# A written-out step order replaced behind its 114th step, in an attention and ELU-MLP kernel

## The chip, the cores and the metric

The kernel runs on one core of one Trainium2 chip. The metric is the device time in microseconds (us), as the median of several runs. One more execution was recorded by the hardware profiler; its instructions, waits and DMA landings are the trace that this document reads.

## The reference

Attention over 8 batches and 8 heads with 576 queries of width 64, causal over 576 keys, and with 16 further "beacon" keys and values per head that every query sees. The heads are put side by side, which gives 4608 tokens of width 512, and these go through a two-layer MLP with an ELU between the layers.

```python
def _attn_ref(q, k, v, beacon_k, beacon_v):
    k_all = np.concatenate([beacon_k, k], axis=2)
    v_all = np.concatenate([beacon_v, v], axis=2)
    scores = scale * np.matmul(q, k_all.transpose(0, 1, 3, 2))
    causal[:, Nb:] = np.triu(np.ones((S, S), dtype=bool), k=1)
    scores = np.where(causal, -1000000000.0, scores)
    ...                                    # softmax over the last axis
    return np.matmul(a, v_all)

x = attn_out.transpose(0, 2, 1, 3).reshape(4608, 512)
h = x @ w_in                               # 512 -> 2048
g = np.where(h > 0.0, h, np.exp(np.minimum(h, 0.0)) - 1.0)
out = g @ w_out                            # 2048 -> 512
```

## The kernel before

The whole kernel is a list of 1554 short steps, written out in one string that `run` goes through. Each step is a small function that issues a few instructions, and a word such as `F.4.11` calls step F with the arguments 4 and 11. No scheduler moves anything afterwards: every engine (PE for matmuls, DVE, ACT, POOL, and SP, which only issues DMAs) executes its own instructions in the order of the list, and stands still while the first of them waits. What a step needs of another engine is held by semaphores that the tile library sets from tiles, their buffers and the order of the list.

Steps by batch b (0 to 7), the attention:

- `lq` (batches 0 to 2) loads q and k with a cast to bf16, and `T`, `cq`, `ck` transpose them on PE and copy them to SBUF. From batch 3 on `lk.b.n` (line 795) copies q (n = 0) or k (n = 1) with a cast into a DRAM scratch tile of its own, and `lt.b.x` (line 802, on SP) brings one half of the heads (x = 0 or 1) back by two DMA transposes, into qst1 (x = 0) or kst1 (x = 1). `lp.b.x` (lines 810 and 811, on POOL) puts the beacon keys and zeros beside them: one memset and one copy.
- `lv.b.j` loads a block of v (line 147; block 0 brings the beacon rows too, line 152). `wi` and `wo` load w_in and w_out. All loads but those of `lt` are issued by POOL, since they cast, and go through one DMA queue (q0). A load also waits on a semaphore for the load eight places ahead of it.
- `S.b.g` (line 330) computes 512 columns of scores into one of two PSUM tiles, `x` (line 345, ACT) takes their exponential, `m` (line 350, DVE) masks them. `D.b.g.n` (line 410) adds blocks on DVE ahead of the sums; `L` computes the softmax sums and part of the product with v, `n` (ACT) their reciprocals, `W` the rest of the product (line 390), `M` (lines 488, 498, 505) scales it into xT, the input of the MLP.

Steps by token tile t (two of 256 tokens, then eight of 512), the MLP:

- `F.t.i` (line 528) computes 512 columns of the first layer into one of two PSUM banks; `e` (line 538) and `u` (line 543) take exponential and ReLU on ACT, `k` (line 553) joins them to the ELU on DVE. Early tiles use `r` and `g` (lines 560 and 566, both DVE) in place of `u` and `k`.
- `G` (line 575) is the second layer of tiles 0 and 1, with `o` and `s` to copy and store. From tile 2 on it is a Strassen-like form with seven products: `Z` and `wt` (line 596, DVE) make sums of activations and weights, `Q.t.a.b` (line 650) issues the matmuls a to b of 112, `J` (lines 664, 668, 671) collects and stores, `Jh` the last two.
- From tile 4 on a part of the first layer has that form as well: `H` and `X` make the sums, `P` (line 732) the products, `K` (lines 742, 745) collects, and `E`, `U`, `V` (lines 754, 761, 771) make the ELU.

The list's order sets everything that can be moved: what POOL issues when, what stands behind what on each engine, and which work is at hand when an engine comes free. Around batch 3, POOL's own order in the list before is

```
lk.3.0 lv.2.0 lk.3.1 lk.4.0 lk.5.0 lv.2.2 lv.2.1 lp.3.1 lv.2.3 lv.3.0 lp.3.0 lk.4.1 lk.7.0 lv.3.1 lv.3.4 lk.6.1
```

and SP's `lt.3.0 s.0.0 lt.3.1 s.0.1 lt.4.0`.

Of the kernel before, what the change touches and what calls it, by code (L numbers as in the profile page):

```python
# [17 lines left out]
def kernel(  # L18
# [837 lines left out]
    wt.3.0 u.2.10 G.1.1.3 M.2.1.0 e.2.8 D.3.0.0 e.2.10 S.3.6 S.3.9 o.1.1 x.3.6 k.2.10 x.3.9 F.2.6
    r.2.8 e.2.6 W.2.1 u.2.6 lv.3.2 k.2.2 S.3.10 lv.3.3 g.2.8 F.2.11 M.2.1.1 F.3.0 x.3.10 o.1.0
    e.2.11 u.2.11 lv.4.0 S.3.8 u.3.0 k.2.6 k.2.11 e.3.0 m.3.0.1 S.3.12 F.3.3 Z.2.3.1 x.3.12 Z.2.3.0
    Z.2.1.1 e.3.3 x.3.8 D.3.0.1 F.3.4 Q.2.0.7 e.3.4 lp.4.0 u.3.4 Q.2.7.14 S.3.11 Z.2.1.0 S.3.7 u.3.3
    Q.2.14.21 J.2.0.v x.3.11 s.0.1 lp.4.1 x.3.7 F.3.13 F.3.14 k.3.4 k.3.3 Q.2.21.28 Z.2.2.0 lv.4.4  # L860
    lt.4.0 e.3.13 S.4.4 Z.2.2.1 u.3.13 S.4.1 lt.4.1 u.3.14 D.3.0.2 D.3.0.3 Q.2.28.35 wt.4.1 lk.5.1
    x.4.4 F.3.8 m.3.1.0 k.3.0 m.3.1.1 x.4.1 e.3.14 s.1.0 L.3.0 W.3.0 F.3.2 n.3.0 k.3.14 M.3.0.0
    M.3.0.1 e.3.8 e.3.2 u.3.8 lv.4.3 Q.2.35.42 S.4.3 S.4.5 u.3.2 J.2.1 lv.4.1 Z.2.4.0 F.3.6 x.4.5
    k.3.8 x.4.3 wt.3.1 k.3.13 lv.4.2 Q.2.42.49 F.3.12 e.3.6 S.4.8 u.3.6 D.3.1.0 S.4.0 x.4.8 X.4.1
    H.4.1 k.3.2 Q.2.49.56 x.4.0 k.3.6 D.3.1.1 F.3.1 Q.2.56.63 u.3.12 J.2.2.v e.3.12 e.3.1 S.4.6
    D.3.1.2 u.3.1 k.3.12 S.4.2 x.4.2 D.3.1.3 F.3.7 x.4.6 F.3.9 e.3.9 lk.6.0 W.3.1 m.4.0.0 e.3.7
    H.3.0 u.3.7 u.3.9 L.3.1 k.3.1 Z.2.4.1 Q.2.63.70 D.4.0.0 k.3.9 F.3.15 n.3.1 M.3.1.1 e.3.15 u.3.15
    F.3.5 Q.2.70.77 M.3.1.0 u.3.5 e.3.5 S.4.12 lt.5.0 S.4.10 lv.5.3 F.3.11 k.3.7 J.2.3 x.4.10
    m.4.0.1 Q.2.77.84 F.4.7 u.3.11 e.3.11 H.4.0 F.3.10 D.4.0.1 k.3.11 x.4.12 k.3.5 J.2.4 S.4.11
    S.4.9 X.4.2 H.4.2 Q.2.84.91 D.4.0.2 e.4.7 Q.2.91.98 u.4.7 Q.2.98.105 e.3.10 J.2.5 P.4.0.0  # L870
    Z.3.3.0 u.3.10 x.4.11 X.4.3 lp.5.0 x.4.9 S.4.7 S.5.3 K.4.0.0 P.4.0.1 P.4.0.2 k.3.15 x.5.3
    K.4.0.1 k.3.10 Q.2.105.112 J.2.6.v P.4.0.3 x.4.7 Q.3.0.7 K.4.0.2 E.4.0.1 S.5.2 S.5.0 P.4.0.4
    K.4.0.3 X.4.4 lp.5.1 lt.5.1 m.4.1.1 k.4.7 x.5.0 P.4.0.5 Z.3.1.0 K.4.0.4 U.4.0.1 Q.3.7.14 x.5.2
    lv.5.4 Q.3.14.21 P.4.0.6 m.4.1.0 lk.7.1 S.5.4 D.4.0.3 U.4.0.6 K.4.0.5 V.4.0.1 E.4.0.6 S.5.5
    F.4.8 x.5.4 F.4.14 x.5.5 J.3.0.v e.4.8 Z.3.2.0 Q.3.21.28 e.4.14 V.4.0.6 u.4.14 L.4.0 W.4.0 u.4.8
    n.4.0 F.4.15 u.4.15 Z.3.3.1 Z.3.1.1 k.4.8 Z.3.4.0 k.4.14 M.4.0.0 F.4.6 Q.3.28.35 Z.3.2.1 e.4.15
    E.4.0.4 F.4.11 u.4.6 M.4.0.1 k.4.15 D.4.1.0 e.4.6 u.4.11 e.4.11 Q.3.35.42 S.5.9 S.5.1 F.4.13
    Z.3.4.1 x.5.9 J.3.1 k.4.11 U.4.0.4 F.4.12 Q.3.42.49 x.5.1 k.4.6 u.4.12 e.4.12 D.4.1.1 e.4.13
    u.4.13 k.4.12 Q.3.49.56 V.4.0.4 S.5.8 D.4.1.2 D.4.1.3 S.5.6 x.5.8 F.4.5 lp.6.0 x.5.6 lv.5.0
    u.4.5 F.4.9 m.5.0.0 Q.3.56.63 k.4.13 e.4.5 lt.6.0 L.4.1 n.4.1 J.3.2.v m.5.0.1 u.4.9 W.4.1 lv.6.3  # L880
    F.4.4 Q.3.63.70 k.4.5 e.4.9 M.4.1.0 lv.5.1 M.4.1.1 F.4.10 S.5.10 X.5.1 u.4.4 k.4.9 S.5.7 e.4.4
    F.5.12 Q.3.70.77 J.3.3 D.5.0.0 X.5.2 e.4.10 Q.3.77.84 E.4.0.5 k.4.4 u.4.10 x.5.7 X.5.4 lv.6.1
    e.5.12 u.5.12 P.5.0.0 x.5.10 Q.3.84.91 K.5.0.0 P.5.0.1 S.5.11 k.4.10 J.3.4 U.4.0.5 S.5.12
    Z.4.3.1 lp.6.1 K.5.0.1 D.5.0.1 P.5.0.2 Q.3.91.98 lt.6.1 Q.3.98.105 J.3.5 x.5.11 lv.5.2 X.5.3
    V.4.0.5 P.5.0.3 D.5.0.2 x.5.12 U.5.0.1 S.6.4 S.6.5 K.5.0.2 lv.6.4 m.5.1.0 x.6.5 Q.3.105.112
    K.5.0.3 P.5.0.4 x.6.4 Q.4.0.7 Z.4.3.0 D.5.0.3 P.5.0.5 K.5.0.4 J.3.6.v S.6.0 E.5.0.1 S.6.3
    Z.4.1.0 P.5.0.6 K.5.0.5 lv.6.2 x.6.3 U.5.0.6 Q.4.7.14 Z.4.2.0 E.5.0.6 L.5.0 n.5.0 F.5.6
    Q.4.14.21 F.5.13 k.5.12 V.5.0.1 e.5.6 m.5.1.1 x.6.0 Q.4.21.28 M.5.0.0 u.5.6 e.5.13 S.6.1 Z.4.1.1
    s.1.1 u.5.13 J.4.0.v S.6.2 V.5.0.6 x.6.2 F.5.4 Z.4.2.1 k.5.13 e.5.4 Q.4.28.35 u.5.4 F.5.15 x.6.1
    D.5.1.0 Q.4.35.42 u.5.15 e.5.15 k.5.6 D.5.1.1 D.5.1.2 F.5.5 lv.6.0 u.5.5 k.5.4 e.5.5 S.6.6 W.5.0  # L890
    J.4.1 k.5.5 U.5.0.5 Z.4.4.1 M.5.0.1 E.5.0.4 F.5.10 U.5.0.4 V.5.0.4 Q.4.42.49 x.6.6 Q.4.49.56
    lt.7.0 S.6.7 D.5.1.3 Z.4.4.0 E.5.0.5 x.6.7 S.6.10 J.4.2.v x.6.10 m.6.0.0 F.5.8 k.5.15 u.5.10
    u.5.8 Q.4.56.63 e.5.10 L.5.1 e.5.8 V.5.0.5 W.5.1 lv.7.1 Q.4.63.70 m.6.0.1 k.5.8 n.5.1 k.5.10
    F.5.14 e.5.14 F.5.7 M.5.1.0 u.5.14 u.5.7 lp.7.0 Q.4.70.77 J.4.3 e.5.7 M.5.1.1 D.6.0.0 S.6.11
    D.6.0.1 S.6.9 x.6.9 F.5.9 e.5.9 k.5.14 F.5.11 Z.5.3.0 u.5.9 x.6.11 e.5.11 X.6.1 u.5.11 X.6.2
    Q.4.77.84 F.6.9 S.6.12 S.6.8 D.6.0.2 lv.7.4 D.6.0.3 Q.4.84.91 J.4.4 F.6.12 X.6.3 x.6.12 x.6.8
    k.5.9 Q.4.91.98 k.5.7 e.6.12 m.6.1.0 S.7.4 u.6.9 S.7.3 Q.4.98.105 u.6.12 P.6.0.0 e.6.9 m.6.1.1
    P.6.0.1 x.7.4 K.6.0.0 Z.5.3.1 Z.5.1.0 x.7.3 J.4.5 Q.4.105.112 P.6.0.2 K.6.0.2 k.5.11 Q.5.0.7
    K.6.0.1 P.6.0.3 J.4.6.v X.6.4 S.7.1 S.7.2 E.6.0.1 U.6.0.1 k.6.9 K.6.0.3 P.6.0.4 x.7.1 Q.5.7.14
    k.6.12 lv.7.0 K.6.0.4 x.7.2 lt.7.1 Z.5.2.0 P.6.0.5 P.6.0.6 V.6.0.1 L.6.0 U.6.0.4 W.6.0 Q.5.14.21  # L900
    K.6.0.5 n.6.0 F.6.5 U.6.0.6 E.6.0.6 F.6.6 E.6.0.4 Q.5.21.28 D.6.1.0 e.6.6 D.6.1.1 u.6.6 M.6.0.1
    J.5.0.v M.6.0.0 Z.5.1.1 V.6.0.4 k.6.6 u.6.5 Z.5.2.1 e.6.5 lv.7.2 S.7.5 S.7.0 Q.5.28.35 x.7.0
    J.5.1 F.6.7 u.6.7 F.6.4 k.6.5 m.7.0.0 Q.5.35.42 e.6.7 k.6.7 u.6.4 F.6.14 Z.5.4.0 x.7.5 D.6.1.2
# [72 lines left out]
```

## Time and profile before

| | us |
|---|---|
| median of 3 runs | 333.67 (333.29 to 335.55) |
| the profiled execution, whole | 334.63 |
| its span, from the first to the last instruction | 332.9 |
| PE busy in it | 321.0 |
| DVE busy | 300.1 |
| ACT busy | 291.6 |
| POOL busy | 89.7 |
| step 115 (S.1.1) starts on PE | 26.6 |
| the last matmul ends | 329.4 |

The predicted time is one of the first row's kind; instruction times and waits are those of the profiled execution, counted from its span's start. The granted TensorE clock was 1.00 throughout. A wait is put down to what released it; "issue" means that the engine waited for nothing that the profile shows.

### The profile page before, as it was taken

The page shows a single profiled execution, that of the slowest core. Times are in us where ns is not written, and L with a number is a line of the kernel's source. Part 1 is how long each engine was busy: PE and PEld are TensorE (multiplying, and loading weights), DVE is VectorE, ACT ScalarE, POOL GpSimd, SP SyncE. Part 2 cuts the span into 40 slices and gives each one's busy share as a digit, 9 for nine tenths or more (in the row PEclk, how much of TensorE's full clock was granted, in tenths as well). Part 3 has the DMA queues.
Part 4 walks back from the last instruction along what each step waited for, and adds up shares of the span by engine and source line. Part 5 has one row for each costly group of instructions (what it writes and reads, how often), then busy time and mean ns, then how long its engine had stood idle before and what let it go on. Part 6 is the DMA issues. An engine that isn't in the chain of part 4 may idle for free. (4 is left out here: it accounts for less than half of the span.)

```text
span 332.9 us, 8762 instructions
## 1 busy us (share of the span) xinstructions
PE 321.0 (96%) x3572; PEld 213.9 (64%) x3575; DVE 300.1 (90%) x568; ACT 291.6 (88%) x481; POOL 89.7 (27%) x121
## 2 busy tenths in 40 slices
...
DMA  8999999999999993592999594510110021020123
GB/s 110 156 179 174 168 186 174 158 149 175 174 158 145 182 165 36 109 137 59 113 126 131 104 59 79 104 34 2 63 35 25 8 96 33 17 81 32 34 79 112
DMA packets 129080, 34.65 MB, mean 104 GB/s; under 512 B 112912, under 2 KB 127504, under 8 KB 129040
## 3 DMA queue, kind: packets, MB, share of 16 engines
q0 software_dynamic: 94912, 18.49, 67.8%
...
q10 hardware_dynamic: 576, 0.13, 0.2%
...
## 5 line engine op out<-in xcount | busy, mean ns | idle before, releaser
L345 ACT ACTIVATE et<-sc 128x1024 f16<-128x1024 f32 (+2 forms) x114 | 105.4, 982 | 2.8 <-PE sc L330 2.3
L528 PE MATMUL hps<-xT,w_in 128*128 128x512 f16 (+1 forms) x448 | 94.9, 349 | 3.6 <-DVE gt L566 2.1
L650 PEld LDWEIGHTS <-gt 128*128 128x128 f16 x768 | 74.2, 98 | 17.7 <-issue 1.9
L528 PEld LDWEIGHTS <-w_in 128*128 128x128 f16 x448 | 41.5, 98 | 37.6 <-issue 7.1
L538 ACT ACTIVATE e<-hps 128x512 f32<-128x512 f32 x96 | 58.3, 622 | 5.9 <-PE hps L528 3.4
L553 DVE SCALAR_TENSOR_TENSOR gt<-e,r 128x512 f16<-128x512 f32 x84 | 56.2, 683 | 1.4 <-ACT r L543 0.7
L543 ACT ACTIVATE r<-hps 128x512 f16<-128x512 f32 x84 | 51.0, 627 | 2.1 <-PE hps L528 1.2
L650 PE MATMUL ops<-w_out,gt 128*128 128x256 f16 x368 | 48.9, 273 | 0.0
L147 POOL DMA_DIRECT2D v<-in_v_dram x40 | 35.8, 949 | 46.9 <-PE ut L390 26.2
L650 PE MATMUL ops<-wt,gt 128*128 128x256 f16 x352 | 48.3, 273 | 0.0
L596 DVE TENSOR_TENSOR gt<-gt 128x1024 f16<-128x1024 f16 x48 | 32.6, 684 | 0.2
L771 DVE SCALAR_TENSOR_TENSOR gt<-e,r 128x512 f16<-128x512 f32 x48 | 32.1, 683 | 0.0
L350 DVE TENSOR_TENSOR et<-et,triu 128x1024 f16<-128x1024 f16 (+5 forms) x66 | 26.9, 447 | 0.5 <-ACT et L345 0.5
L390 PEld LDWEIGHTS <-v 128*32 128x32 f16 (+1 forms) x800 | 17.5, 96 | 10.3 <-issue 2.7
L742 ACT COPY kst<-hps 128x512 f32<-128x512 f32 x36 | 21.6, 601 | 1.9 <-PE hps L732 1.5
L390 PE MATMUL ut<-et,v 128*32 128x464 f16 (+3 forms) x560 | 20.9, 296 | 0.0
L732 PEld LDWEIGHTS <-w_in 128*128 128x128 f16 x192 | 18.4, 98 | 3.4 <-issue 1.2
L410 DVE TENSOR_TENSOR qk<-qk,et 128x1344 f16<-128x1344 f16 (+2 forms) x30 | 17.5, 585 | 0.3
L488 DVE TENSOR_TENSOR xT<-ut,rl 128x672 f16<-128x672 f32 (+12 forms) x26 | 16.4, 670 | 0.6 <-PE ut L390 0.4
L671 DVE TENSOR_TENSOR osb<-ops,sm 128x512 f32<-128x512 f32 x23 | 15.7, 684 | 1.3 <-PE ops L650 1.3
L575 PE MATMUL ops<-w_out,gt 128*128 128x512 f16 x64 | 16.4, 381 | 0.0
L650 PE MATMUL ops<-w_out,s 128*128 128x256 f16 x112 | 15.2, 273 | 0.0
(126 smaller groups left out, 495.2 us busy)
## 6 DMA issues: line engine op xcount, KB each, us to landing
...
```

The costliest lines, as they stand in the source:

```text
L147: nc.gpsimd.dma_start(out=vt[b][r0:r0 + n, j, :, :], in_=v[b, :, ilo[j]:ilo[j] + n, :].rearrange("h s d -> s h d"),)
L345: nc.scalar.activation(out=ets[b, d][:, :, a - EC2 * d:e - EC2 * d], in_=sc[b, g][:, :, a - c0:e - c0], func=AFT.Exp, bias=0.0, scale=SCALE)
L350: nc.vector.tensor_tensor(out=o, in0=o, in1=i, op=ALU.mult)
L390: nc.tensor.matmul(out=t[32 * i:32 * (i + 1), a - qa:e - qa], lhsT=ones[0:kc[j], :] if half is None else v16[0:kc[j], j, h, 32 * half:32 * ...
L528: nc.tensor.matmul(out=h[:, n_, :], lhsT=w_in16[:, cc, P * fc:P * (fc + 1)], rhs=xt[k][:, cc, a - TT * k:e - TT * k], start=(cc == 0), sto ...
L538: nc.scalar.activation(out=eb[t, i], in_=flat(hp[t, i]), func=AFT.Exp, bias=0.0, scale=1.0)
L543: nc.scalar.activation(out=rb[t, i], in_=flat(hp[t, i]), func=AFT.Relu, bias=0.0, scale=1.0)
L553: nc.vector.scalar_tensor_tensor(out=half(t, i), in0=eb[t, i], scalar=1.0, in1=rb[t, i], op0=ALU.subtract, op1=ALU.min)
L596: (nc.vector if eng == "v" else nc.gpsimd).tensor_tensor(out=o_, in0=a_, in1=b_, op=op_)
L650: nc.tensor.matmul(out=xy[t, n_][qd], lhsT=lw[:, P * qd:P * (qd + 1)], rhs=wt_[:, c, :], start=(first and c == 0 and (qd == 0 or (t, n_) n ...
L742: (nc.scalar.copy if eng == "s" else nc.vector.tensor_copy)(out=fm[t, g, ph], in_=src)
L771: eng.scalar_tensor_tensor(out=o_, in0=v_(eb[t, g, ph]), scalar=1.0, in1=v_(rb[t, g, ph]), op0=ALU.subtract, op1=ALU.min)
```

## The change

The first 114 steps stay. The 1440 steps behind them are put in another order: it has the same words, each as often, with the same engines, sizes, tiles and buffer counts. All engines' queues are reordered by it, the loads that POOL issues and the transposes that SP issues among them. In the new list steps of one kind follow each other more often (`F`, `e`, `u`, `k` of one block, all loads of one batch, the eight `D.2` adds with `H.1.2`, `H.2.0` to `H.4.2` near them), and many loads stand earlier. POOL's order around batch 3 becomes

```
wo.2 lk.3.0 wo.3 lk.3.1 lv.2.4 lv.2.0 lv.2.1 lk.6.0 lk.4.1 lv.2.2 lv.2.3 lk.4.0 lk.5.0 lk.7.0 lp.3.1 lp.3.0 lv.3.2 lv.3.0 lv.3.4 lv.3.1 lv.3.3 lk.6.1 lk.7.1 lk.5.1 lp.4.0
```

and SP's `lt.3.0 lt.3.1 s.0.0 s.0.1 s.1.0 lt.4.0`. The diff, cut to the stretch up to batch 3's first scores and to the end:

```diff
-    wh.4 F.0.1 e.0.1 S.1.1 r.0.1 g.0.1 S.1.4 x.1.4 F.0.0 S.1.2 F.0.2 x.1.1 x.1.2 u.0.0 lv.0.3 lv.0.4
-    lq.1.0.4.8 e.0.2 m.0.3.2 m.0.1.2 m.0.3.3 L.0.B n.0.B e.0.0 wi.1.0 wi.1.1 wi.1.2 wi.1.3 wi.1.4
-    wi.1.5 wi.1.6 wi.1.7 W.0.B.0 M.0.B.0 W.0.B.1 M.0.B.1 wo.0 r.0.2 T.1.2.0 F.1.1 ck.1.2.0 g.0.2
-    T.1.3.0 e.1.1 u.1.1 S.1.6 x.1.6 F.0.4 F.1.7 e.0.4 k.0.0 cq.1.3.0 cb.1.3 lq.2.0.0.8 S.1.0 r.0.4
-    S.1.12 e.1.7 g.0.4 r.1.7 F.0.5 x.1.0 S.1.7 g.1.7 x.1.12 H.1.1 cb.2.0 e.0.5 m.1.0.0 r.0.5 wo.1
-    lv.1.4 x.1.7 D.1.0.0 g.0.5 cb.2.2 lv.1.0 F.0.7 S.1.11 e.0.7 r.0.7 x.1.11 G.0.0.0 S.1.9 F.0.3
-    lv.1.1 g.0.7 x.1.9 S.1.10 u.0.3 e.0.3 k.1.1 S.1.8 F.1.6 F.1.3 G.0.1.0 x.1.8 lv.1.3 T.2.3.0 u.1.6
-    x.1.10 T.2.2.0 e.1.3 k.0.3 e.1.6 m.1.0.1 cb.2.1 D.1.0.1 ck.2.3.0 m.1.1.1 ck.2.2.0 m.1.1.0 u.1.3
-    F.1.0 H.1.0 lv.2.4 D.1.0.2 lv.1.2 T.2.1.0 S.2.7 G.0.1.1 D.1.1.0 F.1.2 x.2.7 e.1.0 cq.2.1.0 wo.3
-    D.1.1.1 wo.2 S.2.11 D.1.1.2 k.1.3 D.1.1.3 D.1.0.3 lk.3.0 u.1.0 S.2.12 x.2.11 F.0.6 lv.2.0 x.2.12
-    T.2.0.0 L.1.1 k.1.0 n.1.1 e.0.6 u.1.2 G.0.0.1 e.1.2 cq.2.0.0 M.1.1.0 W.1.1 r.0.6 M.1.1.1 k.1.6
-    g.0.6 W.1.0 L.1.0 F.1.5 F.1.4 n.1.0 lk.3.1 e.1.5 M.1.0.0 M.1.0.1 r.1.5 lk.4.0 e.1.4 r.1.4
-    G.0.1.2 S.2.5 g.1.4 x.2.5 S.2.4 x.2.4 G.0.0.2 lk.5.0 S.2.3 F.2.15 g.1.5 x.2.3 F.2.7 u.2.15
-    wt.1.0 S.2.6 e.2.15 S.2.2 x.2.6 lv.2.2 wt.2.0 lt.3.0 k.1.2 cb.2.3 wt.1.1 G.0.1.3 x.2.2 F.2.0
-    u.2.7 k.2.15 m.2.0.1 e.2.7 S.2.8 u.2.0 wt.2.1 e.2.0 o.0.1 S.2.0 G.0.0.3 x.2.0 F.2.3 F.2.9 lv.2.1
-    e.2.3 x.2.8 o.0.0 lp.3.1 k.2.7 r.2.3 e.2.9 lv.2.3 g.2.3 S.2.9 r.2.9 H.2.1 G.1.0.0 F.2.12 S.2.10
-    x.2.9 g.2.9 S.2.1 e.2.12 u.2.12 x.2.1 x.2.10 G.1.0.1 F.2.13 H.1.2 G.1.0.2 m.2.1.1 s.0.0 lv.3.0
-    F.2.5 u.2.13 k.2.12 e.2.13 lp.3.0 e.2.5 H.2.0 k.2.0 S.3.5 m.2.1.0 S.3.4 D.2.1.0 lk.4.1 G.1.1.0
-    x.3.5 lk.7.0 m.2.0.0 D.2.0.0 F.2.14 u.2.5 F.2.4 lv.3.1 x.3.4 lv.3.4 D.2.0.1 S.3.0 D.2.0.2 e.2.14
 ...
-    P.9.3.5 Q.9.0.8 V.9.2.5 K.9.3.4 P.9.3.6 U.9.3.1 U.9.3.4 K.9.3.5 J.8.5 U.9.3.5 E.9.3.5 E.9.3.6
-    V.9.3.1 Z.9.2.0 U.9.3.6 E.9.3.4 Q.8.98.105 V.9.3.5 Z.9.3.1 Q.9.8.16 Q.8.105.112 Q.9.16.24 J.9.0
-    V.9.3.6 V.9.3.4 Q.9.24.32 Q.9.32.40 Z.9.1.1 Z.9.2.1 J.9.1 Q.9.40.48 Q.9.48.56 Z.9.4.0 J.9.2
-    J.8.6 Q.9.56.64 Z.9.4.1 Q.9.64.72 J.9.3 Q.9.72.80 J.9.4 Q.9.80.88 Q.9.88.96 Q.9.96.104 J.9.5
-    Q.9.104.112 Jh.9.0 Jh.9.1
+    wh.4 F.0.1 e.0.1 m.0.3.3 wi.1.2 lv.0.3 m.0.1.2 lv.0.4 cb.1.3 wi.1.4 wi.1.6 H.1.1 H.1.0 r.0.1
+    lq.1.0.4.8 wi.1.7 m.0.3.2 wi.1.3 wi.1.0 wi.1.1 wi.1.5 wo.0 lq.2.0.0.8 lv.1.1 wo.1 lv.1.0 g.0.1
+    lv.1.4 lv.1.2 lv.1.3 wo.2 lk.3.0 wo.3 lk.3.1 F.0.2 e.0.2 S.1.4 r.0.2 cb.2.1 x.1.4 g.0.2 L.0.B
+    n.0.B W.0.B.0 M.0.B.0 S.1.2 x.1.2 F.0.0 S.1.1 x.1.1 u.0.0 e.0.0 W.0.B.1 M.0.B.1 lv.2.4 lv.2.0
+    lv.2.1 lk.6.0 k.0.0 lk.4.1 lv.2.2 lv.2.3 lk.4.0 lk.5.0 lk.7.0 T.1.2.0 ck.1.2.0 F.1.1 e.1.1 u.1.1
+    T.1.3.0 cq.1.3.0 H.1.2 S.1.6 x.1.6 F.0.4 e.0.4 r.0.4 F.1.7 e.1.7 g.0.4 S.1.0 r.1.7 cb.2.0 g.1.7
+    m.1.0.1 x.1.0 S.1.12 x.1.12 F.0.5 e.0.5 r.0.5 k.1.1 g.0.5 m.1.0.0 S.1.11 S.1.7 x.1.11 x.1.7
+    F.0.7 e.0.7 r.0.7 g.0.7 D.1.0.0 cb.2.2 D.1.0.1 D.1.0.2 G.0.0.0 S.1.10 S.1.9 cb.2.3 x.1.10 x.1.9
+    m.1.1.0 D.1.0.3 F.0.3 e.0.3 u.0.3 k.0.3 G.0.1.0 S.1.8 x.1.8 m.1.1.1 D.1.1.0 F.1.6 u.1.6 T.2.2.0
+    e.1.6 ck.2.2.0 T.2.3.0 ck.2.3.0 F.1.3 e.1.3 u.1.3 F.1.0 e.1.0 u.1.0 T.2.1.0 cq.2.1.0 D.1.1.1
+    k.1.6 D.1.1.2 D.1.1.3 S.2.7 wt.1.0 x.2.7 G.0.1.1 F.1.2 S.2.12 x.2.12 S.2.11 x.2.11 u.1.2 F.0.6
+    e.0.6 T.2.0.0 cq.2.0.0 k.1.3 L.1.1 n.1.1 e.1.2 M.1.1.0 r.0.6 lp.3.1 G.0.0.1 W.1.1 L.1.0 n.1.0
+    M.1.1.1 k.1.0 lp.3.0 M.1.0.0 g.0.6 F.1.5 e.1.5 r.1.5 W.1.0 lv.3.2 M.1.0.1 lv.3.0 lv.3.4 g.1.5
+    wt.2.0 lv.3.1 lv.3.3 lk.6.1 lk.7.1 lk.5.1 lt.3.0 lt.3.1 S.2.5 x.2.5 F.1.4 e.1.4 r.1.4 wt.1.1
+    g.1.4 wt.2.1 k.1.2 wt.4.0 G.0.1.2 S.2.4 wt.4.1 x.2.4 S.2.3 x.2.3 F.2.15 u.2.15 e.2.15 G.0.0.2
+    S.2.2 x.2.2 F.2.3 e.2.3 r.2.3 F.2.7 k.2.15 u.2.7 S.2.6 e.2.7 g.2.3 k.2.7 x.2.6 S.2.0 m.2.0.1
+    x.2.0 G.0.0.3 o.0.0 F.2.0 e.2.0 u.2.0 s.0.0 F.2.9 k.2.0 e.2.9 r.2.9 g.2.9 S.2.8 x.2.8 S.2.9
+    x.2.9 H.2.0 H.2.1 m.2.1.1 G.0.1.3 o.0.1 s.0.1 F.2.12 u.2.12 e.2.12 G.1.0.0 S.2.10 H.2.2 x.2.10
+    m.2.1.0 S.2.1 x.2.1 H.4.1 m.2.0.0 H.4.2 k.2.12 D.2.0.0 D.2.1.0 D.2.0.1 F.2.5 e.2.5 u.2.5 k.2.5
+    D.2.1.1 D.2.0.2 H.4.0 D.2.1.2 D.2.0.3 D.2.1.3 F.2.13 e.2.13 u.2.13 k.2.13 G.1.1.0 S.3.5 x.3.5
+    S.3.4 x.3.4 F.2.14 e.2.14 u.2.14 k.2.14 G.1.1.1 G.1.0.1 S.3.1 x.3.1 wt.3.0 S.3.0 x.3.0 F.2.4
 ...
+    Q.8.56.63 P.9.3.0 K.9.3.0 U.9.2.5 Q.8.63.70 J.8.3 P.9.3.1 K.9.3.1 V.9.2.5 Q.8.70.77 Z.9.3.0
+    P.9.3.2 K.9.3.2 E.9.3.1 Z.9.1.0 U.9.3.1 Q.8.77.84 J.8.4 P.9.3.3 K.9.3.3 P.9.3.4 K.9.3.4 U.9.3.4
+    E.9.3.4 V.9.3.1 Q.8.84.91 P.9.3.5 K.9.3.5 U.9.3.5 E.9.3.5 Q.8.91.98 J.8.5 V.9.3.4 V.9.3.5
+    Z.9.3.1 P.9.3.6 U.9.3.6 E.9.3.6 V.9.3.6 Z.9.1.1 Q.9.0.8 Z.9.2.0 Q.9.8.16 Q.9.16.24 Z.9.2.1 J.9.0
+    Q.8.98.105 Z.9.4.0 Q.9.24.32 J.9.1 Z.9.4.1 Q.8.105.112 J.8.6 Q.9.32.40 Q.9.40.48 J.9.2 Q.9.48.56
+    Q.9.56.64 J.9.3 Q.9.64.72 Q.9.72.80 J.9.4 Q.9.80.88 Q.9.88.96 J.9.5 Q.9.96.104 Jh.9.0
+    Q.9.104.112 Jh.9.1
```

More of the change, by code (lines that the diff above doesn't have):

```diff
@@ L856 @@
[L856 to L903, printed above, removed]
@@ new lines @@
+    D.3.0.0 F.2.8 e.2.8 r.2.8 F.2.10 e.2.10 u.2.10 k.2.10 S.3.6 g.2.8 lt.4.0 x.3.6 m.3.0.1 D.3.0.1
+    S.3.9 x.3.9 lp.4.0 G.1.1.3 F.2.6 e.2.6 W.2.1 lv.4.3 u.2.6 M.2.1.1 k.2.6 D.3.0.2 Z.2.3.0 lv.4.2
+    o.1.1 lv.4.0 D.3.0.3 s.1.1 wt.3.1 lv.4.1 lv.4.4 S.3.10 x.3.10 F.2.11 u.2.11 e.2.11 Z.2.3.1
+    k.2.11 Z.2.1.1 Z.2.1.0 F.3.0 e.3.0 u.3.0 k.3.0 S.3.12 S.3.8 x.3.8 x.3.12 F.3.4 e.3.4 u.3.4 k.3.4
+    F.3.3 e.3.3 u.3.3 Q.2.0.7 S.3.11 x.3.11 S.3.7 k.3.3 m.3.1.1 x.3.7 m.3.1.0 lp.4.1 lt.4.1 Q.2.7.14
@@ new lines @@
+    F.3.13 e.3.13 Z.2.2.0 u.3.13 k.3.13 Q.2.14.21 F.3.14 Z.2.2.1 S.4.1 x.4.1 S.4.4 x.4.4 J.2.0.v
+    Q.2.21.28 e.3.14 Z.2.4.0 F.3.8 L.3.0 n.3.0 u.3.14 u.3.8 M.3.0.0 e.3.8 W.3.0 M.3.0.1 D.3.1.0
+    k.3.8 k.3.14 X.4.1 Q.2.28.35 J.2.1 D.3.1.1 Z.2.4.1 D.3.1.2 D.3.1.3 F.3.2 e.3.2 u.3.2 S.4.3 x.4.3
+    S.4.5 k.3.2 x.4.5 F.3.12 e.3.12 u.3.12 k.3.12 F.3.6 Q.2.35.42 u.3.6 S.4.0 S.4.8 x.4.8 x.4.0
+    m.4.0.0 e.3.6 k.3.6 Q.2.42.49 J.2.2.v F.3.1 e.3.1 u.3.1 Q.2.49.56 S.4.6 lp.5.0 S.4.2 k.3.1 x.4.2
+    x.4.6 H.3.0 lt.5.0 m.4.0.1 Q.2.56.63 F.3.9 u.3.9 e.3.9 F.3.7 L.3.1 D.4.0.0 u.3.7 n.3.1 k.3.9
```

115 lines of the change are left out of this document (74 added, 41 removed).

## The prediction

> **What bounds the kernel now.** I read the page first (busy times, slices, queues), then the windows of 10 us, the waits of POOL, the POOL timeline and the landings of single loads, and last the two ends of the trace.
>
> ```profile
> span 332.9 us, 8762 instructions
> PE 321.0 (96%) x3572; PEld 213.9 (64%) x3575; DVE 300.1 (90%) x568; ACT 291.6 (88%) x481; POOL 89.7 (27%) x121
> DMA  8999999999999993592999594510110021020123
> q0 software_dynamic: 94912, 18.49, 67.8%
> ```
> ```profile
> 80.00:90.00 10.00, 10.00 (x83) 4.07 (x84) 9.86 (x17) 9.77 (x15) 5.74 (x4) 1.00 1.97 171
> 180.00:190.00 10.00, 10.00 (x107) 5.93 (x104) 9.97 (x17) 9.61 (x18) 0.00 (x0) 1.00 0.33 69
> ```
>
> A window's row gives its length and then the busy us of PE, PEld, DVE, ACT and POOL. PE, DVE and ACT are all nearly full, at a granted clock of 1.00. A busy PE may only be pipelined, so I add up its work by what one step adds before the next one starts: F 0.87 us, a Q of seven matmuls 0.76, P 0.44, S 0.33, W 1.4, and so on. Behind step 114 that makes 299 us, and PE really goes from 26.6 (S.1.1) to 329.4 us (the last Q): 302.8. So PE waits for about 4 us in all, some 2.9 of them before 60 us and the rest at the end. PE sets the time; **a new order can gain at most these 4 us, and loses whatever it makes PE wait.** The step lists hold the same names, so the work of every engine stays.
>
> The DMA row shows engines full for the first 110 us, by GpSimd's queue q0 above all. So I looked there for what a moved load does.
>
> ```profile
> POOL scr L795 <- issue: 16.4, 4, 4.6
> ```
> ```profile
> 55.15 3.26 POOL L795 DMA_DIRECT2D scr<-in_q_dram  x1
> 63.00 2.19 POOL L795 DMA_DIRECT2D scr<-in_q_dram  x1 [4.59 <-issue]
> ...
> 66.45 0.69 POOL L810 MEMSET kst<- 128x96 bf16 x1
> 66.57 0.85 POOL L811 COPY kst<-bkT 128x32 bf16<-128x32 bf16 x1
> ...
> 69.93 0.20 POOL L810 MEMSET qst<- 128x96 bf16 x1
> 70.05 0.23 POOL L811 COPY qst<-bkT 128x32 bf16<-128x32 bf16 x1
> 74.80 2.20 POOL L795 DMA_DIRECT2D scr<-in_k_dram  x1 [4.51 <-issue]
> 81.62 2.20 POOL L795 DMA_DIRECT2D scr<-in_q_dram  x1 [4.62 <-issue]
> ```
>
> These are lk.4.0, lk.5.0, lp.3.1, lp.3.0, lk.4.1 and lk.7.0. Three lk issues (and a fourth, lk.6.1 at 88.07) stood 2.6 to 4.6 us with POOL idle and no semaphore to wait for. The landings tell why:
>
> ```profile
> L795 POOL DMA_DIRECT2D scr<-in_q_dram x1: 2207/2207/2207, 50.4 to 50.4; - x1
> ...
> DMA to landing us min/median/max: 12.3/12.3/12.3
> ```
>
> This is lk.3.0: issued 50.40, landed 62.7, and lk.5.0 starts at 63.0. In the same way lk.4.0 landed at 74.5 (lk.4.1 starts 74.8), lk.5.0 at 81.3 (lk.7.0 starts 81.6), lv.3.0 at 87.85 (lk.6.1 starts 88.07). An lk is 576x8 = 4608 pieces of 128 bytes in the code, and the trace has 4533 to 4663 packets of q0 between landings that bracket one; a lv of 128 rows is 1024, of 80 rows 640. Counting what was issued and not landed, the queue took an lk when that made 15,872 pieces (lk.4.0, the two wo counted at 512 each) and held one that would have made 16,512, until a whole earlier load had landed. So **q0 lets some 16 thousand pieces in, about three lk, and the POOL instruction that doesn't fit blocks all behind it.** Loads land in order: alone an lk takes 3.7 us (lk.4.1, 87.85 to 91.57), beside SP's transposes 7.1 and 6.8.
>
> **The change part by part.** (1) *Loads.* In the old order lk.3.0, 3.1, 4.0, 5.0 stand before lp.3.1 and lp.3.0. In the new one lk.3.0, 3.1, 6.0, 4.1, 4.0, 5.0 and 7.0 do, and lp.3.0 writes beacon columns that S.3.4 on PE waits for in both orders. Worked out from the landings:
>
> - Up to the last lv.1 the same pieces are in q0; lv.1.2 landed at 52.96 with lv.2.4 (0.4 us) ahead of it, which now comes later.
> - Old, 52.96 to 81.31: two wo, lv.2.0 and four lk. New, up to the landing of lk.4.1: two wo, lv.2.0, four lk (3.0, 3.1, 6.0, 4.1), lv.2.4 (cancels) and lv.2.1 (0.8). That is 82.1.
> - On SP the transposes lt.3.1 (issued at 73.73 and 75.47) lose the store ahead of them and follow lt.3.0 at once. Four transposes and two stores cost the loads about 10 us in the old order (two lk 3.4 and 3.1 over 3.7, five lv the rest); of the last transpose (2.4 us) about half moves ahead: +1.1, so lk.4.1 lands at 83.2.
> - lk.6.0 fits once lk.3.0 has landed, lk.4.1 after lk.3.1, lk.4.0 at once, lk.5.0 after lk.6.0. For lk.7.0 the queue holds lk.4.1, lk.4.0, lk.5.0 and two lv: 15,872, so it waits for lk.4.1: 83.2 + 0.3 = 83.5.
> - The next POOL instruction starts 1.7 behind an lk (63.00 to 64.68); lp.3.1 takes 1.0 (66.45 to 67.42), lp.3.0 0.35: S.3.4 may start at 86.6.
>
> S.3.5 and S.3.4 are this row; S.3.4 started at 80.65, and 0.8 us less PE work stands ahead of it now, so it would start at 79.9:
>
> ```profile
> 80.41 0.62 PE L330 MATMUL sc<-qst 64*128 64x144 bf16 x10
> ```
>
> PE stands **86.6 - 79.9 = 6.7 us**; behind S.3.4 wait F.2.14, G.1.1.1 and all of PE, then ACT's x.3.4 and DVE's masks. Bounds: 4.5 if the transposes cost nothing more (82.1, and POOL's next step overlaps by 1 us more), 10 if all four and the stores come ahead (86).
>
> (2) *Later loads.* S.4.1 waits for lt.4.0, which goes when S.3.6 is done and landed 13.25 us later (94.69 to 107.94; S.4.4 started at 108.04, just behind). The PE work between S.3.6 and the first S.4 is 13.1 us old and 13.0 new, now beside three lk. I take +0.4, between 0 and 1.5. Loads before lk.3.0 move past each other, but T.1.2 (lq.1, its k now at 32.7, needed 33.7), F.0.4 (wi.1, 35.9, needed 37.6) and L.1.1 (lv.1, 52.6, needed 57) keep cover of 1.0 to 4 us; gone, each would cost PE its lateness.
>
> (3) *DVE.* Masks and H.1 now fill waits of this kind:
>
> ```profile
> 27.29 0.69 DVE L560 SCALAR_TENSOR_TENSOR r<-e,ones 128x512 f16<-128x512 f32 x1 [4.11 <-ACT e L538]
> 32.61 1.80 DVE L505 TENSOR_TENSOR xT<-ub,rl 128x512 f16<-128x512 f32 x4 [3.11 <-ACT rl L454]
> ```
>
> About 2 us of DVE are gained there. Then all eight adds D.2 (1.12 + 0.85 + 0.59 + 0.32 for each half, 5.8 us), masks and H.4 stand nearly together ahead of k.2.13: by sums of DVE and PE work DVE's place in the list falls 8 us back against PE's between G.1.0.0 and F.2.13, and M.2.1.1 would reach F.3.0 2.9 us late. While PE stands 6.7 us at S.3.4, DVE catches up, so I count 0; without the stall it is worth about 1 us more than the lateness that the old order has there (1.9). H, wt and X elsewhere go with it: same instructions, DVE is behind PE by about the same sums in the later stages.
>
> (4) *The end.* From P.9.3.6 on PE has 126 Q matmuls of 0.109 us left, before 118; the old order waited for Z at 321.3, the new one less: 0, between -1 and +1.
>
> [...]
>
> **Sum.** 6.7 + 0.4 = 7.1. The profiled execution took 334.63 (span 332.9 and 1.7 around it): 341.7. The median of the runs is 0.96 under it, so **340.8 us**, with 338 to 345 from the bounds.
>
> **Rivals.** *No hold* (0.14): q0 takes the five lk without a stop, since its limit was only inferred from four waits. Then five issues of 2.2 to 3.3 us end by about 75, lp.3.0 is ready before 79.9, and only DVE's burst is left: +1, 334.7. For it: the limit itself is in no row; against it: every one of the waits ends 0.2 to 0.3 us behind a landing. *Faster* (0.04): as before without hold, and DVE's two filled waits also take away what PE loses before 60 us, 2.9: 330.8 or, with some of the end, 330. It decides if S.3.4 starts before 80 and M.2.1.1 isn't late; the sums for M.2.1.1 speak against it. *Worse* (0.08): the hold comes twice, lk.6.1, 7.1 and 5.1 standing together ahead of lp.4.0 and beside lt.4.0, which then lands as late as a lt behind 7 us lks: 4 us more at S.4.1 and lk.4.1 landing at 86: 333.67 + 10 + 4 = 347.7. The forecast has 0.74.
>
> **Chances.** 1% is 3.3 us, about what a measurement of this kernel can tell from no change: 330.3 to 337.0. No hold lies within it, as does a little of the forecast's lower end: 0.14 same; faster 0.04; slower 0.82. The range for 8 in 10 runs from 335.0 (between no hold and the forecast) to 346.0.
>
> **What would show it.** In the new profile: POOL waits of "issue" before lk.5.0 and lk.7.0, the latter until 83 to 84 with lk.4.1 landing just before; lp.3.0's copy ending near 86.5; a PE wait of 5 to 9 us at S.3.4 with POOL's qst copy as its releaser, and ACT idle with it; a shift that stays until the end. Wrong: lp.3.0 before 80, lk.7.0 issued without a wait, or PE standing elsewhere (L.2.0, F.3.0 behind DVE; S.4.1 behind lt.4.0; the late K and P steps).

## The result, and the profile after

The changed kernel takes 342.67 us (342.57 to 344.50) beside 334.65 us for the kernel before on the same chip: a ratio of 1.024, 95% interval 1.021 to 1.027, some 8 us slower. The forecast was 340.8, in a range from 335 to 346. It rested on a median before of 333.67 us from three runs, which six runs put at 334.65. Its size came out close because a stall that ended earlier than worked out and a slow clock that was not in the sum partly cancel, and the reason it gave was one of two that each would have done.

The page of the kernel after, with the lines that answer to those shown of before (PEclk is the granted clock in 40 slices of 8.5 us):

```profile
span 341.0 us, 8783 instructions
PE 324.4 (95%) x3575; PEld 213.5 (63%) x3575; DVE 300.7 (88%) x568; ACT 289.8 (85%) x481; POOL 93.0 (27%) x121
PEclk9999999997699999999999999999999999999999
q0 software_dynamic: 94912, 18.49, 65.0%
```

The work is the same, but two slices show a slow clock, between 76 and 94 us. PE's timeline around them (start, duration, engine, line, operation, the idle time before it):

```profile
76.75 0.39 PE L330 MATMUL sc<-qst 64*128 64x144 bf16 x6
85.61 0.61 PE L330 MATMUL sc<-qst 64*128 64x192 bf16 x4 [8.46 <-POOL qst L811]
86.15 1.89 PE L528 MATMUL hps<-xT,w_in 128*128 128x512 f16 x4
```

The first row is S.3.5, the second S.3.4, the third F.2.14. Ahead of S.3.4 PE stands 8.46 us for POOL's qst copy (lp.3.0); F.2.14 then takes 1.89 us, twice what a block of F added up to before. The windows of this stretch (length, then the busy us of PE, PEld, DVE, ACT, POOL, then the granted clock, DMA share and GB/s):

```profile
78.00:80.00 2.00, 0.00 (x0) 0.00 (x0) 2.00 (x3) 1.11 (x2) 0.00 (x0) 1.00 1.79 221
80.00:82.00 2.00, 0.00 (x0) 0.00 (x0) 2.00 (x4) 0.00 (x0) 0.00 (x0) 0.56 1.91 231
88.00:90.00 2.00, 2.00 (x7) 0.64 (x5) 0.69 (x1) 1.08 (x2) 1.83 (x3) 0.50 2.47 158
90.00:92.00 2.00, 2.00 (x13) 0.67 (x12) 0.69 (x1) 0.60 (x1) 0.67 (x1) 0.88 2.46 157
```

PE is empty from 77.1 on, the clock falls to a half at 80.2, while PE idles, and comes back at 90.5, nearly 5 us after PE has work again. POOL's timeline shows what the copy waited for, and the landing of lk.4.1 (the row of 63.82) how long the last hold went:

```profile
63.82 2.19 POOL L795 DMA_DIRECT2D scr<-in_k_dram  x1 [4.57 <-issue]
...
75.46 2.20 POOL L795 DMA_DIRECT2D scr<-in_q_dram  x1 [5.47 <-issue]
82.78 2.19 POOL L795 DMA_DIRECT2D scr<-in_q_dram  x1 [5.12 <-DVE kst L410]
...
84.57 0.73 POOL L811 COPY kst<-bkT 128x32 bf16<-128x32 bf16 x1
...
85.28 0.28 POOL L811 COPY qst<-bkT 128x32 bf16<-128x32 bf16 x1
```
```profile
L795 POOL DMA_DIRECT2D scr<-in_k_dram x1: 2187/2187/2187, 63.8 to 63.8; - x1
...
DMA to landing us min/median/max: 18.7/18.7/18.7
```

lk.4.1 was issued at 63.82 and landed 18.7 us later, at 82.5; lk.7.0 starts at 82.78. The profile puts that wait down to a D add of DVE, with which an lk has nothing to do; the landing is the cause, as it is for lk.5.0 at 75.46 (lk.6.0 landed at 75.15).

**Where 8.0 us come from.** Both profiled executions, 334.63 and 342.67 us, followed step by step: S.3.4 could have started at 77.0 in the new order, not at 79.9; -2.9. Of these, 0.8 us are no gain of the order: PE's first matmul behind step 114 starts at 25.7 instead of 26.6 us, although the steps before it are the same, and over all runs below it starts between 25.5 and 27.4. The other 2 are the new order's own gain. The stall is +8.6 (77.0 to 85.61), so that S.3.4 comes 5.7 us behind its old place. From S.3.4 to L.2.0, the same PE work in every run of this order, it took 10.1 us, with the clock at 0.50 until 90.48, and 8.1 in e1 and f3 below, where it is 1.00: +2.0. The last +0.3 lies in the 240 us behind L.2.0 and was not followed further. That is 8.0.

### The profile page after: what moved, and what is told of

The parts are those of the page before. It is cut to its first block, busy times and chain, and to the rows that moved or that the text cites. A ratio compares the mean times of both kernels' runs of the same rounds, so it can differ in the third digit from the quotient of the medians.

```text
span 341.0 us, 8783 instructions
## 1 busy us (share of the span) xinstructions
PE 324.4 (95%) x3575; PEld 213.5 (63%) x3575; DVE 300.7 (88%) x568; ACT 289.8 (85%) x481; POOL 93.0 (27%) x121
## 4 chain that ended last, share of the span: by engine, by line
PE 61%; ACT 12%; issue 9%; DVE 6%; POOL 6%; DMA 5%; ACTq 0%; DVEq 0%; POOLq 0%
PE ops L650 22%; PE hps L528 15%; PE hps L732 10%; ACT et L345 7%; PE sc L330 4%; DMA w_out<-in_moe_w_out_dram 4%; PE ut L390 4%; POOL scr L795 3%; ACT r L543 2%; PE ut L650 2%; PE ops L575 2%; ACT e L538 2%; POOL v L147 1%; DVE qk L410 1%; DVE gt L553 1%
## 5 line engine op out<-in xcount | busy, mean ns | idle before, releaser
L528 PE MATMUL hps<-xT,w_in 128*128 128x512 f16 (+1 forms) x448 | 96.0, 352 | 1.1 <-DVE gt L566 0.8
L538 ACT ACTIVATE e<-hps 128x512 f32<-128x512 f32 x96 | 60.5, 643 | 3.9 <-PE hps L528 2.1
L528 PEld LDWEIGHTS <-w_in 128*128 128x128 f16 x448 | 40.8, 98 | 36.0 <-issue 6.0
L543 ACT ACTIVATE r<-hps 128x512 f16<-128x512 f32 x84 | 53.3, 651 | 1.4 <-PE hps L528 1.2
L650 PE MATMUL ops<-w_out,gt 128*128 128x256 f16 x368 | 48.2, 273 | 0.0
L650 PE MATMUL ops<-wt,gt 128*128 128x256 f16 x352 | 47.6, 273 | 0.0
L732 PEld LDWEIGHTS <-w_in 128*128 128x128 f16 x192 | 18.3, 97 | 4.8 <-issue 1.6
L330 PE MATMUL sc<-qst 64*128 64x336 bf16 (+13 forms) x160 | 11.6, 255 | 8.6 <-POOL qst L811 8.5
L575 PE MATMUL ops<-w_out,gt 128*128 128x512 f16 x64 | 17.5, 405 | 0.0
```

The costliest lines, as they stand in the source:

```text
L528: nc.tensor.matmul(out=h[:, n_, :], lhsT=w_in16[:, cc, P * fc:P * (fc + 1)], rhs=xt[k][:, cc, a - TT * k:e - TT * k], start=(cc == 0), sto ...
L538: nc.scalar.activation(out=eb[t, i], in_=flat(hp[t, i]), func=AFT.Exp, bias=0.0, scale=1.0)
L543: nc.scalar.activation(out=rb[t, i], in_=flat(hp[t, i]), func=AFT.Relu, bias=0.0, scale=1.0)
L650: nc.tensor.matmul(out=xy[t, n_][qd], lhsT=lw[:, P * qd:P * (qd + 1)], rhs=wt_[:, c, :], start=(first and c == 0 and (qd == 0 or (t, n_) n ...
L732: nc.tensor.matmul(out=hx[t, g, n_][:, c, :], lhsT=lw, rhs=rh, start=(first and c == 0 and k_ == 0), stop=(k_ == 1), skip_group_check=True)
```

## The experiments

All times are medians; the ratio is to the kernel before on the same chip (334.4 to 335.0 us).

| run | edit | us | ratio (95%) |
|---|---|---|---|
| e1 | after; lk.5.0, lk.7.0 behind lp.3.0 | 337.57 | 1.008 (1.005 to 1.011) |
| e4 | after; only lk.7.0 behind lp.3.0 | 343.09 | 1.024 (1.021 to 1.027) |
| e2 | after; 36 matmuls fill the stall | 341.32 | 1.019 (1.016 to 1.022) |
| e3 | before; lk.4.1, lk.7.0 early | 341.19 | 1.017 (1.012 to 1.021) |
| f1 | e4 with memsets for lp's copies | 334.78 | 1.000 (0.998 to 1.002) |
| f2 | after with memsets for lp's copies | 343.15 | 1.027 (1.023 to 1.031) |
| f5 | e4 with three short DVE memsets | 342.09 | 1.022 (1.019 to 1.025) |
| g1 | e4 with two longer rows of DVE memsets | 336.27 | 1.002 (0.999 to 1.006) |
| f3 | after; lk spread behind the lp steps | 332.61 | 0.993 (0.991 to 0.996) |
| f4 | before with the new first stretch | 333.55 | 0.995 (0.992 to 0.998) |

**e1: both held loads behind the beacon columns.**

```diff
-lk.4.0 lk.5.0 lk.7.0 ... lp.3.1 ... lp.3.0 M.1.0.0
+lk.4.0 ... lp.3.1 ... lp.3.0 lk.5.0 lk.7.0 M.1.0.0
```

> The changed order with one edit: lk.5.0 and lk.7.0 are issued right behind lp.3.0 instead of ahead of lp.3.1. Theory A (the hold of q0 alone makes the change slower, and the stall at S.3.4 brings the drop of the TensorE clock with it): lp.3.0 ends by about 71 us, S.3.4 starts at about 77 when PE gets to it, PE does not stand there, the granted clock stays at 1.00 from 80 to 92 us, and of the 8.5 us of stall and some 2.3 us of slow clock about 10 go: 331 to 334 us, a little under the kernel before. Rival B (the compute order, DVE's D.2 burst above all, costs the time and the hold is in the way of nothing else): PE stands at L.2.0, F.3.0 or another DVE-fed step for most of what it stood at S.3.4, 338 us or more.

S.3.4 went at 76.3 with no stall and the clock at 1.00 there, as A has it; the total missed A's range by 3.6 us. The PE wait had moved on to S.4.1 (3.4 us) and took one stretch of slow clock with it. A row of PE's waits and POOL's timeline say why:

```profile
PE sc L330 <- POOL qst L811: 3.4, 1, 3.4
```
```profile
102.94 2.19 POOL L795 DMA_DIRECT2D scr<-in_k_dram  x1 [4.87 <-PE ops L650]
...
104.73 1.96 POOL L811 COPY qst<-bkT 128x32 bf16<-128x32 bf16 x1
```

lk.5.1 stands ahead of lp.4.0. It was held until lv.3.4 had landed at 102.58. Two lk and two lv of 1024 pieces were then still on their way, with lk.5.1 15,872; lv.3.4 would have made it 16,512. These are the two numbers of the prediction, once more. What was new: the copy behind it took 1.96 us, longer than any in the kernel before (0.21 to 1.62).

**e4: half of it.**

```diff
-lk.5.0 lk.7.0 ... lp.3.1 ... lp.3.0 M.1.0.0
+lk.5.0 ... lp.3.1 ... lp.3.0 lk.7.0 M.1.0.0
```

> The changed order with one edit, half of that in the run before it: only lk.7.0 goes behind lp.3.0, lk.5.0 stays ahead of lp.3.1. Theory A (a load that does not fit blocks POOL until a whole earlier load has landed; for lk.5.0 that is lk.6.0 at about 75.2 us): lk.5.0 is issued at about 75.5, lp.3.0 ends at about 78.6, S.3.4 starts at about 78.8 where PE gets to it at 77.1: 1.5 to 2 us of stall, too short for the clock to fall, 333 to 335 us. Rival (the hold is a matter of each single lk, so that the half edit takes half of the time): S.3.4 at about 81, 337 to 339 us.

A's first step came true (lk.5.0 at 75.52) and its result did not: 343.09 us, no better than the change. Rows of POOL, then the last row of DVE in this stretch:

```profile
77.34 8.11 POOL L811 COPY kst<-bkT 128x32 bf16<-128x32 bf16 x1
...
85.51 0.20 POOL L811 COPY qst<-bkT 128x32 bf16<-128x32 bf16 x1
```
```profile
84.70 0.68 DVE L553 SCALAR_TENSOR_TENSOR gt<-e,r 128x512 f16<-128x512 f32 x1
```

A copy of 32 columns took 8.11 us and ended at 85.45. From 75.6 to 85.38 DVE had run masks, H, `k` and D.2 without a gap, all instructions that read two SBUF operands; with the last of them the copy ended. So a second theory, L: POOL's copy, which reads SBUF, waits as long as DVE runs such instructions. The next runs test it. The clock fell here as well (0.83 in the window from 80 to 82 us, 0.50 from 82 to 90). That a stall of 1.5 to 2 us is too short for this, as theory A has it here and theory L at f5, was the author's estimate; f1's slow clock behind 1.76 us speaks against it.

**f1: the same with nothing to read.** lp's second instruction becomes a memset, so that this kernel leaves out the beacon keys of batches 3 to 7.

```diff
-        nc.gpsimd.tensor_copy(out=t[:, :, 1, 0:NB], in_=bkT[:, 2 * x_:2 * x_ + 2, NB * b:NB * (b + 1)])
+        nc.gpsimd.memset(t[:, :, 1, 0:NB], 0.0)
```

> As the run in which only lk.7.0 goes behind lp.3.0, but the copy in lp is a memset of the same columns (the beacon keys of batches 3 to 7 are left out, zeros stand in their place), so that POOL writes there and reads nothing from SBUF. Theory L (a POOL copy is kept waiting as long as DVE runs instructions with two inputs in SBUF back to back: the kst copy took 8.11 us and ended at 85.45, DVE's last such instruction at 85.38): lp.3.0 ends 0.5 us after lk.5.0's issue, at about 77.8, S.3.4 starts by 78.2, PE stands there 1 us or less and the clock stays at 1.00. What is left is a stall behind lp.4.0, as where both lk go behind lp.3.0, less some 1.5 us since its copy is not kept either: 334 to 337 us. Rival H (POOL stood for q0 or for its own program between 77 and 85): lp.3.0 stays at about 85.5, 342 to 344 us.

POOL's rows for the two memsets, and the windows behind them:

```profile
77.91 0.64 POOL L811 MEMSET kst<- 128x32 bf16 x1
...
78.09 0.64 POOL L811 MEMSET qst<- 128x32 bf16 x1
```
```profile
78.00:80.00 2.00, 1.21 (x7) 0.46 (x8) 2.00 (x3) 1.76 (x3) 0.73 (x5) 0.79 1.55 204
80.00:82.00 2.00, 2.00 (x6) 0.69 (x5) 2.00 (x4) 1.18 (x3) 0.00 (x0) 0.50 1.68 255
```

Beside the same DVE chain both end by 78.73, and the run is 8 us faster than e4. So here a POOL instruction that reads nothing was not kept (0.64 us beside 8.11); whether it is the read, or another difference between a copy and a memset, no run here shows. Theory L's stall and clock missed: lk.6.0 landed at 75.79, PE stood 1.76 us (77.03 to 78.79), and this short stall was enough for a clock of 0.50 from 79.2 to 82.6.

**f2: the hold alone.** The memset of f1 in the changed order itself.

> The changed order itself with the memset in place of lp's copy (beacon keys of batches 3 to 7 left out, zeros in their place); all loads where the change has them. It takes the wait for DVE away and leaves the hold of q0. Theory H and L together (each alone keeps S.3.4 until about 85): lk.7.0 is held until lk.4.1 has landed, 82.5, lp.3.0 ends at about 84.9 instead of 85.56, S.3.4 starts 0.5 to 0.8 us earlier than with the copy, the stall and the slow clock stay: 341 to 343 us. Rival (only the wait for DVE counts): S.3.4 by 79, 334 to 337 us.

lk.7.0 was held until 83.86, lp.3.0 ended at 86.48, S.3.4 started at 86.53 where PE had ended S.3.5 at 77.96: 8.6 us of stall, 343.15 us. From lk.7.0's issue to the end of lp.3.0 it took 2.62 us, in the changed kernel 2.78: there the wait for DVE added 0.2. The total lies just above what was expected, and S.3.4 was not earlier but later, since lk.4.1 landed 1.1 us later in this run. So **each of the two causes keeps S.3.4 until about 85**, and taking one away gains nothing. The second one is not wholly apart from the first: in e4 it is lk.5.0's own hold, until 75.5, that puts lp.3 into DVE's chain.

**f5 and g1: breaks in DVE's chain.** f5 puts a memset of 64 columns behind m.2.0.0, H.4.2 and k.2.12; g1 five of 256 columns behind m.2.0.0 and behind k.2.12.

```diff
-... m.2.0.0 H.4.2 k.2.12 D.2.0.0 ...
+... m.2.0.0 dz H.4.2 dz k.2.12 dz D.2.0.0 ...      (f5: one memset each)
+... m.2.0.0 dz H.4.2 k.2.12 dz D.2.0.0 ...         (g1: five memsets each)
```

> As the run in which only lk.7.0 goes behind lp.3.0, copies as they were; DVE gets three short memsets of 64 columns (dz), behind m.2.0.0, H.4.2 and k.2.12, in the middle of its chain of instructions with two SBUF inputs. Nothing else changes and no work is left out. Theory L: at each of them POOL gets its turn, the kst copy ends at about 77.9 and the qst copy at 78.4 to 78.8, S.3.4 starts at about 79, PE stands 1.5 to 2 us, too short for the clock to fall: 335 to 338 us with the stall behind lp.4.0 that is left. Rival 1 (the copy waits for more than a short break, or for DVE to be idle): S.3.4 at 85.7, 342 to 344 us. Rival 2 (D.2's adds alone keep POOL, and those begin at 78.6): as theory L, but without the dz the copies would have ended before 78.6, which the earlier run speaks against.

Rival 1 it was: the three memsets took 0.09 us each, the next instruction started beside them, the kst copy (the last two memsets fell into its time) stood from 78.45 to 84.14, S.3.4 started at 85.11. It ended at a boundary between two D and H instructions that both read two SBUF operands, so POOL got in at this boundary, and at those before it from 78.45 on not; what sets it apart is open.

> As the run with short memsets in DVE's chain, but at two places only (behind m.2.0.0 and behind k.2.12), and each is five memsets of 256 columns in a row, some 0.6 to 0.8 us by the 0.09 us that one of 64 columns took, in which DVE reads nothing from SBUF. lk.7.0 goes behind lp.3.0, lk.5.0 stays ahead. Theory L (POOL's reading copy gets in as soon as DVE is for some tenths of a us without two SBUF inputs; the breaks of 0.09 us, which the next instruction overlapped, were too short): the kst copy ends in the first break, near 78.5, the qst copy in the second, near 79.6; S.3.4 starts at about 79.8 instead of 85.1 to 85.8, PE stands 2 to 3 us and the clock is low for one stretch of 3.4 us: 334 to 338 us. Rival (POOL waits for an idle DVE or for something else that ends at about 85): S.3.4 at 84 or later, 341 us or more.

Rows of g1 (its lines are one higher), POOL and then DVE:

```profile
75.28 2.70 POOL L812 COPY kst<-bkT 128x32 bf16<-128x32 bf16 x1
...
75.55 2.69 POOL L812 COPY qst<-bkT 128x32 bf16<-128x32 bf16 x1
```
```profile
77.25 0.68 DVE L351 TENSOR_TENSOR et<-et,triu 128x1024 f16<-128x1024 f16 x1
77.91 1.20 DVE L817 MEMSET gap<- 128x128 uint32 x5
```

Both copies end in the first break, at 77.98 and 78.24, the mask ahead of it at 77.93. S.3.4 started at 78.30, nearly 7 us earlier than in f5, for 2.4 us of added DVE work. PE stood 0.7 us and the clock stayed at 1.00, less than expected, since both copies got through in the first break. The total (336.27) is within what was expected, though lk.5.0 was held only until 73.47 here.

**e2: the stall filled.**

```diff
-... S.3.5 x.3.5 S.3.4 ...
+... S.3.5 x.3.5 wz.36 S.3.4 ...      (36 matmuls of 512 columns)
```

> The changed order with 36 matmuls of 512 columns added on PE just ahead of S.3.4, into a PSUM bank that nothing reads; they take about 7.7 us and lie inside the stall of 8.5 us. Theory A (PE's own idling makes the granted clock fall to 0.50, which costs about 2.3 us behind the stall): the clock stays at 1.00 from 80 to 92 us, S.3.4 still starts at about 85.6, and the time is 340 to 341 us although PE has 7.7 us more work. Rival B (the clock falls for another reason, the heat or the DMA load of that stretch): the clock falls all the same, 342 to 344 us. Rival C (the stall at S.3.4 is no wait for POOL but PE work that the trace lacks): the 7.7 us add to the time, 349 to 351 us.

The window that answers to that of 88 us above:

```profile
88.00:90.00 2.00, 2.00 (x11) 0.89 (x10) 0.00 (x0) 2.00 (x3) 1.57 (x3) 1.00 2.45 157
```

The clock stayed at 1.00 with the DMA share as it was (2.45 beside 2.47), so PE's idling lowers it, not the loads: rival B falls. From S.3.4 to L.2.0 PE took 7.8 us instead of 10.1. C falls too: 7.7 us more work made it no slower. The total, 341.3, is a little above A's range. The profiled execution (342.32) began 1.6 us later on PE than that of the change, and lk.4.1 landed 1.9 us later; whether the other runs did so too, no trace shows.

**e3: a hold in the old order.**

```diff
-lk.5.0 ... lp.3.0 ... lk.4.1 ... lk.7.0
+lk.5.0 lk.4.1 lk.7.0 ... lp.3.0 ...
```

> The kernel before with one edit: lk.4.1 and lk.7.0 are issued right behind lk.5.0, ahead of lv.2.2, lv.2.1, lp.3.1, lv.2.3, lv.3.0 and lp.3.0; no compute step moves. Theory A (the hold of q0 by itself is enough to make the old compute order slower): the two lk and lv.2.3 fill q0, POOL stands until lk.5.0 has landed at about 81.6, lp.3.0 ends at about 84, S.3.4 goes from 80.65 to about 84.3, and later steps start as much later: 337 to 340 us. Rival B (nothing is held when the compute order is the old one): S.3.4 at 80.7, 333 to 335 us.

Slower by 1.7%, a little above A's range, and not where A has it. lk.4.1 stood until lk.3.1 and lk.7.0 until lk.4.0 had landed; lv.2.3 stood until lk.5.0 had, already at 77.0. lp.3.0 ended at 80.1 and S.3.4 started at 80.2. PE stood 2.4 us in W.2.0 instead, since the loads of v that it needs landed behind the moved lk, the last of them (lv.2.3) at 92.8. The profiled execution (337.84) was the shortest of four, the others took 341 us; where these lost 3 us more is open.

**f3: the loads spread out.** From POOL's order of the change:

```diff
-lk.4.0 lk.5.0 lk.7.0 lp.3.1 lp.3.0 lv.3.2 ... lv.3.3 lk.6.1 lk.7.1 lk.5.1 lp.4.0 ... lp.4.1 ... lp.5.0
+lk.4.0 lp.3.1 lp.3.0 lv.3.2 ... lv.3.3 lk.5.0 lp.4.0 lk.5.1 ... lp.4.1 lk.6.1 ... lp.5.0 lk.7.0 lk.7.1
```

> The changed order with the early loads spread behind the lp steps: lk.5.0 behind lv.3.3, lk.5.1 behind lp.4.0, lk.6.1 behind lp.4.1, lk.7.0 and lk.7.1 behind lp.5.0; no compute step moves. Theory (hold and lock at lp.3 and lp.4 are all that the new order loses): S.3.4 at about 77 as in the run with lk.5.0 and lk.7.0 behind lp.3.0 (337.6 us), and lp.4.0 ends before PE comes to S.4.1 at about 103.5, so that its stall of 3.4 us and 1.2 us of slow clock go as well: 331 to 334 us, 1 to 3 us under the kernel before. Rival (the lost time moves on to the next place, lp.4.0 or lp.4.1 kept waiting by DVE, or lt.5.0 late): 336 us or more.

```profile
span 331.3 us, 8783 instructions
PEclk9999999999999999999999999999999999999999
```

332.61 us, as expected: 10 us under the changed kernel and 0.7% (0.4 to 0.9) under the one before, no stall of PE over 1.3 us, S.3.4 at 77.55, S.4.1 at 105.1. With five words of 1554 moved, the new compute order is the faster one.

**f4: the new first stretch on the old order.** The compute steps up to D.1.0.3 come from the new list, the rest and all lk and lv.2 from the old.

> The kernel before, with the changed order's compute steps for the first stretch behind step 114 only (up to D.1.0.3, PE's first 25 us or so behind it); lk and lv.2 stay where the old order has them, and all later steps keep the old order. Theory (the new order's gain lies in this stretch, where masks and H.1 fill two waits of DVE: PE's starts less the sum of its work rise by 1 to 1.4 us there, not by 3): lp.3.0 and S.3.4 as early as in the old order, no stall there, 332 to 333.5 us, 1 to 2 us under the kernel before. Rival (the early waits come back later, since DVE or ACT set the time behind that stretch in the old order): 334 to 335 us, no difference.

333.55 us, 0.5% (0.2 to 0.8) under the kernel before. PE's start less the sum of its work rises from 26.9 to 29.2 us over its first 60 us of work, by 2.3, where before has 3.3 and f3 1.8. So 1.0 of the 1.5 us that f3 gains by then lies in this stretch; the rest comes behind it.

## Why the prediction was right, and where not

- **Loads, +6.7.** The hold came as worked out: lk.5.0 held for lk.6.0, lk.7.0 for lk.4.1, which landed at 82.5 (83.2 predicted); lp.3.0 done at 85.56, S.3.4 at 85.61 (86.6). As a stall the term measured 8.6: its end was worked out 1.0 too late and its start 2.9 too late (79.9 was the old place less 0.8 us of work). What it adds to the total is S.3.4's start against that old place, 5.7 instead of 6.7.
- **The start of that term** is a step that failed, though it cost the total nothing here: the landing of lk.4.1 sets when S.3.4 goes, so a PE that comes earlier only waits longer. The sum priced what the moves cost PE later and nothing of what they give it earlier, although step (3) itself counted 2 us that DVE gains. In DVE's timeline of the kernel after, the waits of 4.11 and 3.11 us have become these, and PE gained some 2 us by 76 us; in f3, which does not stall there, the last matmul ends 1.6 us ahead of the kernel before, with a start 0.5 ahead.

```profile
25.67 0.29 DVE L596 TENSOR_TENSOR lo<-w_in 128x256 f16<-128x256 f16 x1 [1.73 <-DMA v<-in_v_dram]
...
32.50 0.69 DVE L505 TENSOR_TENSOR xT<-ub,rl 128x512 f16<-128x512 f32 x1 [1.78 <-PE ub L390]
```

- **S.4.1, +0.4.** Nothing: lt.4.0 landed at 114.33, and PE came there at 114.7.
- **DVE's burst, 0.** It cost PE nothing here, but "without the stall about 1 us" was wrong by far: e4 shows that the burst, once lp.3 falls into it, keeps lp.3 for 8.11 us and PE for 8.4. I had looked at who waits for DVE's results, not at POOL's copies, of which the one in e4 ended at 85.45, with DVE's chain at 85.38. The D adds did not lengthen lk.7.0's issue: it took 2.19 us beside them.
- **The clock, not in the sum:** +2.0. This is the term that the sum lacked and that counts: a stall was priced at its length alone.
- **The end, 0:** from P.9.3.6 on it took 14.46 us with 126 Q matmuls, before 14.02 with 118. Eight Q are 0.87 us, so the end waits 0.4 us less, within the bounds of 1.
- **Rivals.** *Faster* with 330.8 needed S.3.4 before 80 and M.2.1.1 not late; f3 meets both and takes 332.6, so it was the right picture of this order without its loads. *No hold* fell with the POOL rows. *Worse* was right that the hold would come back at lp.4.0 (e1), but in the changed kernel PE was too late to notice.

So the place and the reason of the stall were right, and 5.7 of the 8.0 us came that way. That the total is near is in part luck: the 2.0 of the slow clock, which the sum lacked, made up for the 1.0 by which the stall ended earlier and the 0.4 that did not come at S.4.1. The second cause, which kept S.3.4 as late in e4, where lk.7.0's hold is gone, was not seen at all.
